# Seven pieces of zeros for an output: three written inside the attention loop, four behind it

## Chip, cores and metric

The kernel runs on one core of a Trainium2 chip. The metric is the device time of one execution in microseconds (us); smaller is better.

## What is computed

Two steps follow each other. The first is a decaying linear attention over 4 batches, 8 heads, 768 positions and head size 64; the second is a mixture of experts, in which each of the 3,072 resulting rows of 512 values goes through its two best of eight experts.

```python
for t in range(S):
    state = gamma * state + einsum('bhd,bhe->bhde', k[:, :, t], v[:, :, t])
    y[:, :, t] = scale * einsum('bhd,bhde->bhe', q[:, :, t], state)
x = y as rows of (batch, position), 512 wide
logits = x @ w_gate + log1p(exp(x @ w_noise)) * noise
top2 = the two largest of 8 logits; top2_w = their softmax
for e in range(8):
    for k in range(2):
        mask = top2[:, k] == e
        h = maximum(x[mask] @ w1[e], 0)
        out[mask] += top2_w[mask, k] * (h @ w2[e])
```

## The kernel before

**The attention loop** (lines 758 to 791) goes over 24 chunks of 128 positions, six per batch. For each chunk TensorE makes the scores, the output and the new state, and transposes the rows; the rows go to a DRAM buffer `xbuf` in half precision (`x_store`, line 424). Into the loop's chunks a table of jobs is woven: `at(j, f, ...)` (line 661) puts a job at the end of chunk j. So the loads and conversions of the first experts' weights and the routing of the first three batches (`route_a` to `route_w`) run beside the attention.

**Zeros.** The results of the experts are added into the output by indirect transfers with an add, so the output has to be zero first. A tile `zero` in SBUF holds zeros, and `zero_out(i)` (line 300) writes one piece of the output from it: pieces 0 to 5 are two transfers of 512 KB each (line 304, one for each half of the output), piece 6 is two of 128 KB (line 308). Lines 739 and 740 put the seven pieces at the ends of chunks 12, 14, 16, 18, 20, 21 and 22.

**Behind the loop** (from line 1017) the routing of the last batch runs, while TensorE already works on expert 0: `early(n)` takes the next n units of a list of its matmuls. Around the change the code stands in this order: the gathers and transposes of the rows that batch 2 gave expert 0 (lines 1049 to 1052), the two loads of expert 1's second weights (lines 1054 and 1055, 1 MiB each), then `route_a` to `route_e` of the last batch. In between, `route_w(b - 1)` (line 1070) writes the gate rows of batch 2 from `gateb` into a DRAM table `gbuf` (line 526), and `gates(0, 3, ...)` (line 1071) gathers gate rows from it.

**Queues.** Nothing reorders instructions: each engine runs its own in the order of the code. SP (SyncE) issues loads, stores, zeros, the writes into `gbuf` and the transposes of gathered rows (`x_t`, line 701). GpSimd (POOL) issues all indirect transfers: the gathers of x rows from `xbuf` (`gather`, line 679), of gate rows from `gbuf` (`gates`, line 689) and the adds into the output (`put`, line 964). SP's transfers signal their landing on eight counters in turn (`DMAHW0_49` to `DMAHW7_49`), GpSimd's on eight others (`DMASW0_49` to `DMASW7_49`). Before SP issues a transfer on a counter, it waits until the transfer that used this counter last has landed, which is the one eight places ahead.

**Expert 1** is the first whose products go by `mm1s` (line 872). Its `out_scale` (line 941, called by `hook` at step 11) multiplies the gathered gate rows of all its seven blocks (line 951, VectorE); it needs the last gate gather of expert 1.

Of the kernel before, what the change touches and what calls it, by code (L numbers as in the profile page):

```python
# [96 lines left out]
def moe_kernel(ctx, tc, qT, kT, kt, vt, noise, wgn, w1, w2, ctab, qtab, xbuf, gbuf, out):  # L97
# [22 lines left out]
    def K(n):  # L120
        return ct[:, _C[n][0]:_C[n][1]]
# [178 lines left out]
    def zero_out(i):  # L300

        if i < 6:
            for o in out:
                nc.sync.dma_start(o[128 + i * 512:128 + (i + 1) * 512, :].rearrange("(p r) d -> p r d", p=128),
                                  zero[:, None, :HD].to_broadcast([128, 4, HD]))
        else:
            for o in out:
                nc.sync.dma_start(o[:128, :], zero[:, :HD])
# [139 lines left out]
    def route_a(b):  # L448
        sl = slice(b * NC, (b + 1) * NC)
        nc.vector.tensor_scalar(invp[b % 2].bitcast(I32), upx[:, sl].bitcast(I32), -1.0, float(254 << 23),  # L450
                                op0=OP.mult, op1=OP.add)
        lg = work.tile([128, NC, 2 * E], F32, name="lg")
        nc.vector.tensor_copy(lg, PL[:, :, 1])
        nc.vector.tensor_tensor(lg, lg, PL[:, :, 0], op=OP.add)
        nc.vector.scalar_tensor_tensor(lg, lg, gx, invp[b % 2][:, :, None].to_broadcast([128, NC, 2 * E]),
                                       op0=OP.mult, op1=OP.mult)
        sp = work.tile([128, NC, E], F32, name="sp")
        nc.scalar.activation(sp, lg[:, :, E:], AF.Exp)
        nc.scalar.activation(small.rearrange("p (c e) -> p c e", c=NC), sp, AF.Ln, bias=1.0)
        R[b] = lg  # L460

    def route_b(b):

        lg, sp = R[b], small.rearrange("p (c e) -> p c e", c=NC)
        o = int(b >= B0)
        ny = work.tile([128, NC, NY], F32, name="ny")
        nc.vector.tensor_tensor(sp, sp, nz[:, b * NC:(b + 1) * NC, :], op=OP.mult)
        nc.vector.memset(ny[:, :, 0:1] if o else ny[:, :, E:NY], -3.0e38)
        nc.vector.tensor_tensor(ny[:, :, o:o + E], sp, lg[:, :, :E], op=OP.add)
        oh = work.tile([128, 2, NC, NL], F32, name="oh", bufs=B)  # L470
        m8 = work.tile([128, NC, 8], F32, name="m8")
        i8 = work.tile([128, NC, 8], U32, name="i8")
        for c in range(NC):
            nc.vector.max(m8[:, c, :], ny[:, c, :])
        for c in range(NC):
            nc.vector.max_index(i8[:, c, :], m8[:, c, :], ny[:, c, :])
        R[b] = (oh, m8, i8)
# [183 lines left out]
    def at(j, f, *a):  # L661
        todo.setdefault(j, []).append((f, a))
# [73 lines left out]
    at(23, w_scaled, nc.scalar, 0, "2", 0)  # L736
    at(22, w_load, 1, "1", 0, 2)
    at(22, w_load, 1, "1", 2, 2)
    for i in range(7):
        at((12, 14, 16, 18, 20, 21, 22)[i], zero_out, i)  # L740
    at(2, nc.vector.tensor_copy, lanes16, K("lanes"))
    at(2, nc.vector.tensor_copy, blks16, K("blks"))
    at(2, nc.vector.tensor_copy, lanes.bitcast(F32), lanes16.bitcast(F32))
# [279 lines left out]
    def early(n):  # L1023
        for _ in range(n):
            if units:
                units.pop(0)()
# [28 lines left out]
    w_load(1, "2", 2, 2)  # L1055
    early(1)
    route_a(b)
    early(1)
    route_b(b)
    early(1)  # L1060
# [275 lines left out]
```

## Time and profile before

| what | value |
|---|---|
| median of 3 runs | 647.22 us (646.4 to 648.09) |
| the profiled execution | 647.68 us, its span 645.9 us |
| TensorE busy | 621.1 us, 96% of the span |
| VectorE, ScalarE, GpSimd busy | 446.4, 391.8, 399.3 us |
| moved by DMA | 112.88 MB, mean 175 GB/s |

The loop ends at about 123 us of the span; the rest is the experts. Busy times count instructions of an engine that overlap nothing else of it. Between brackets behind an instruction of the timeline stands how long its engine was idle before it, and what ended that ("issue": nothing that the profile shows). PEclk is the granted clock of TensorE as a share of 2.4 GHz, its other level being 1.2 GHz.

### The profile page before, as it was taken

What the parts mean: (1) busy time and instruction counts of PE and PEld (TensorE: products, weight loads), DVE (VectorE), ACT (ScalarE), POOL (GpSimd) and SP (SyncE); (2) the same over time, 40 slices, a digit from 0 to 9 for tenths busy, and PEclk for the clock granted to TensorE, in tenths of its full rate; (3) what the DMA queues carried; (4) which work ended last, traced back from release to release, by engine and by line L of the source; (5) the groups of instructions that cost most, each with busy time, mean ns of one, the idle gap of its engine ahead of it and who ended that gap; (6) DMA issues with size and microseconds to landing.
All of it is one profiled execution on the core that took longest, in us unless ns stands there. A gap on an engine that the chain in (4) does not pass through costs nothing.

```text
span 645.9 us, 12856 instructions
## 1 busy us (share of the span) xinstructions
PE 621.1 (96%) x4949; PEld 387.3 (60%) x4949; DVE 446.4 (69%) x947; ACT 391.8 (61%) x655; POOL 399.3 (62%) x279
## 2 busy tenths in 40 slices
PE   7999998899899999999999999999999999999995
PEld 4888887655656544654465446544654465445784
DVE  4568988477767799379827983798369656957730
ACT  4687986763356765576547755765576557656311
POOL 3455998254768756884488468736865774583164
PEclk9999999899999999999999999999999999999999
DMA  9899999953955597459745964695477649732043
GB/s 331 314 390 400 352 379 350 303 185 105 214 73 157 86 209 245 51 121 201 206 54 107 253 167 52 112 251 165 54 156 197 165 51 165 187 44 34 6 53 44
DMA packets 107248, 112.88 MB, mean 175 GB/s; under 512 B 64496, under 2 KB 84080, under 8 KB 103600
## 3 DMA queue, kind: packets, MB, share of 16 engines
q1 hardware_dynamic: 86080, 84.29, 44.4%
q0 software_dynamic: 20528, 26.90, 26.0%
q8 instruction: 40, 0.66, 0.4%
q10 hardware_dynamic: 576, 0.84, 0.3%
q14 instruction: 24, 0.20, 0.1%
HBM read 72.16 MB, written 26.47 MB: 153 GB/s over the span
## 4 chain that ended last, share of the span: by engine, by line
PE 81%; DVE 9%; DMA 3%; ACT 2%; POOL 2%; issue 2%; another core or an unknown queue 1%; SPq 0%; POOLq 0%; ACTq 0%
PE pO L990 11%; PE pO L988 10%; PE pO L989 10%; PE pH L889 9%; PE pH L887 9%; PE pH L888 9%; PE pY L378 3%; PE pA L365 3%; PE pY L384 3%; DVE h L904 2%; PE pX L418 2%; PE pU L394 2%; PE pO L979 1%; PE pO L977 1%; PE pO L978 1%
## 5 line engine op out<-in xcount | busy, mean ns | idle before, releaser
L964 POOL DMA_INDIRECT out<-ot,idx x108 | 197.2, 1826 | 144.9 <-ACT ot L958 59.6
L990 PE MATMUL pO<-w2h,h 128*128 128x512 f16 x336 | 127.4, 379 | 2.5 <-DVE h L904 2.5
L988 PE MATMUL pO<-w2h,h 128*128 128x512 f16 x336 | 127.3, 379 | 0.1
L989 PE MATMUL pO<-w2l,h 128*128 128x512 f16 x336 | 127.3, 379 | 0.0
L911 DVE TENSOR_TENSOR s<-pH,s 128x416 f32<-128x416 f32 (+2 forms) x84 | 47.1, 573 | 49.7 <-PE pH L889 32.2
L689 POOL DMA_INDIRECT gx<-gbuf,idx x54 | 61.7, 1142 | 27.7 <-issue 14.6
L679 POOL DMA_INDIRECT xg<-xbuf,idx x55 | 60.0, 1091 | 22.7 <-issue 14.3
L958 ACT ACTIVATE ot<-pO,gse 128x512 f32<-128x512 f32 (+2 forms) x48 | 32.6, 682 | 58.9 <-PE pO L990 54.5
L191 ACT ACTIVATE junk<-wst 128x1024 bf16<-128x1024 f32 x64 | 67.8, 1059 | 0.0
L903 ACT ACTIVATE h<-s 128x832 f16<-128x832 f32 (+2 forms) x42 | 36.3, 872 | 39.9 <-DVE s L911 32.5
L907 ACT ACTIVATE s<-pH 128x416 f32<-128x416 f32 (+2 forms) x84 | 40.3, 508 | 32.6 <-PE pH L889 29.8
L990 PEld LDWEIGHTS <-h 128*128 128x128 f16 x336 | 32.8, 98 | 44.0 <-DVE h L904 5.0
L988 PEld LDWEIGHTS <-h 128*128 128x128 f16 x336 | 32.9, 98 | 38.7 <-ACT h L903 0.6
L887 PE MATMUL pH<-xt,wsh 128*128 128x416 f16 (+2 forms) x168 | 56.0, 333 | 0.2 <-DVE h L904 0.2
L989 PEld LDWEIGHTS <-h 128*128 128x128 f16 x336 | 32.9, 98 | 38.8
L889 PE MATMUL pH<-xt,wsl 128*128 128x416 f16 (+2 forms) x168 | 56.0, 333 | 0.0
L888 PE MATMUL pH<-xt,wsh 128*128 128x416 f16 (+2 forms) x168 | 56.0, 333 | 0.0
L220 DVE SCALAR_TENSOR_TENSOR w2l<-wst,wsc,w2h 128x1024 f16<-128x1024 f32 x28 | 35.8, 1279 | 14.1 <-ACT w2h L215 10.0
L338 POOL TENSOR_TENSOR vp<-in_v,ct 128x512 f32<-128x512 f32 x24 | 25.0, 1043 | 31.0 <-issue 16.8
L904 DVE SCALAR_TENSOR_TENSOR h<-s,h 128x832 f16<-128x832 f32 (+2 forms) x42 | 41.5, 990 | 2.3 <-ACT h L903 2.3
L845 ACT ACTIVATE xt<-s 128x832 f16<-128x832 f32 (+2 forms) x28 | 24.5, 874 | 28.6 <-DVE s L844 28.3
L372 DVE TENSOR_TENSOR am<-pA,ct 128x512 f32<-128x512 f32 x48 | 30.9, 684 | 14.6 <-PE pA L365 12.1
(216 smaller groups left out, 1489.8 us busy)
## 6 DMA issues: line engine op xcount, KB each, us to landing
wst<-w SPq DMA_DIRECT2D x28, 1024.0 KB
in_q<-qT SPq DMA_DIRECT2D x24, 256.0 KB
in_k<-kT SPq DMA_DIRECT2D x24, 256.0 KB
in_v<-vt SPq DMA_DIRECT2D x24, 256.0 KB
xbuf<-xr SPq DMA_DIRECT2D x24, 256.0 KB
out<-zero SPq DMA_DIRECT2D x12, 512.0 KB
in_kt<-kt SPq DMA_DIRECT2D x20, 256.0 KB
wst<-w SPq DMA_DIRECT2D x8, 512.0 KB
```

The lines of the kernel that those rows point to most:

```text
L191: nc.scalar.activation(junk, st[:, i * 1024:(i + 1) * 1024], AF.Square, accum_out=ss[:, i:i + 1])
L679: nc.gpsimd.indirect_dma_start(out=x[:p1], out_offset=None, in_=xbuf[:128 + rows], in_offset=bass.IndirectOffsetOnAxis(ap=idx[:p1, i:i + 1 ...
L689: nc.gpsimd.indirect_dma_start(out=GX[e][:, t, :], out_offset=None, in_=gbuf[:128 + rows], in_offset=bass.IndirectOffsetOnAxis(ap=idx[:, i ...
L887: nc.tensor.matmul(p, wh, bh[:, k, :], start=start and k == 0, stop=False, skip_group_check=True)
L888: nc.tensor.matmul(p, wh, bl[:, k, :], start=False, stop=False, skip_group_check=True)
L889: nc.tensor.matmul(p, wl, bh[:, k, :], start=False, stop=(k == 1), skip_group_check=True)
L904: wait.append(lambda: nc.vector.scalar_tensor_tensor(lo, src, 0.0, hi, op0=OP.max, op1=OP.subtract))
L911: nc.vector.tensor_tensor(s[:, u], p, s[:, u], op=OP.add)
L964: nc.gpsimd.indirect_dma_start(out=out[s], out_offset=bass.IndirectOffsetOnAxis(ap=idx[:n, i:i + 1], axis=0), in_=ot[:n, s * HD:(s + 1) * ...
L988: nc.tensor.matmul(p, a, WT["2h"][:, f, :], start=(f == 0), stop=False)
L989: nc.tensor.matmul(p, a, WT["2l"][:, f, :], start=False, stop=False)
L990: nc.tensor.matmul(p, c, WT["2h"][:, f, :], start=False, stop=(f == FT - 1))
```

## The change

Three pieces of zeros stay in the loop, now at the ends of chunks 12, 15 and 18. The other four (three pairs of 512 KB and the pair of 128 KB) are issued behind the loop, after `route_a` of the last batch.

```diff
@@ -736,8 +736,8 @@
     at(23, w_scaled, nc.scalar, 0, "2", 0)
     at(22, w_load, 1, "1", 0, 2)
     at(22, w_load, 1, "1", 2, 2)
-    for i in range(7):
-        at((12, 14, 16, 18, 20, 21, 22)[i], zero_out, i)
+    for i in range(3):
+        at((12, 15, 18)[i], zero_out, i)
     at(2, nc.vector.tensor_copy, lanes16, K("lanes"))
@@ -1055,6 +1055,8 @@
     w_load(1, "2", 2, 2)
     early(1)
     route_a(b)
+    for i in range(3, 7):
+        zero_out(i)
     early(1)
     route_b(b)
```

The order of SP at the loop's end, before: `x_store` (L424), the transposes of expert 0's first rows (L701), zeros (L304, L308) and the loads of expert 1's first weights (L187).

```order
L304 DMA out<-zero 512x1x256 [waits DMAHW6_49]
L304 DMA out<-zero 512x1x256 [waits DMAHW7_49]
L424 DMA xbuf<-xr 128x1024 [waits DMAHW0_49,Activation_49]
L701 DMA_TRANSPOSE xe<-xg 128x8x128 [waits DMAHW1_49,DMASW0_49]
L701 DMA_TRANSPOSE xe<-xg 128x8x128 [waits DMAHW2_49,DMASW1_49]
L701 DMA_TRANSPOSE xe<-xg 128x8x128 [waits DMAHW3_49,DMASW2_49]
L304 DMA out<-zero 512x1x256 [waits DMAHW4_49]
L304 DMA out<-zero 512x1x256 [waits DMAHW5_49]
L424 DMA xbuf<-xr 128x1024 [waits DMAHW6_49,Activation_49]
L187 DMA wst_2217<-w 128x2048 [waits DMAHW7_49,Pool_49]
L187 DMA wst_2217<-w 128x2048 [waits DMAHW0_49]
L308 DMA out<-zero 128x256 [waits DMAHW1_49]
```

The same place of SP now:

```order
L424 DMA xbuf<-xr 128x1024 [waits DMAHW3_49,Activation_49]
L424 DMA xbuf<-xr 128x1024 [waits DMAHW4_49,Activation_49]
L701 DMA_TRANSPOSE xe<-xg 128x8x128 [waits DMAHW5_49,DMASW0_49]
L701 DMA_TRANSPOSE xe<-xg 128x8x128 [waits DMAHW6_49,DMASW1_49]
L701 DMA_TRANSPOSE xe<-xg 128x8x128 [waits DMAHW7_49,DMASW2_49]
L424 DMA xbuf<-xr 128x1024 [waits DMAHW0_49,Activation_49]
L187 DMA wst_2211<-w 128x2048 [waits DMAHW1_49,Pool_49]
L187 DMA wst_2211<-w 128x2048 [waits DMAHW2_49]
```

The zeros around the transposes and behind the weight loads are gone from here; the rest keeps its order.

The order of SP behind the loop, before: the transposes of expert 0's next rows, the loads of expert 1's second weights, the write of the gate table (L526), the next transposes.

```order
L701 DMA_TRANSPOSE xe<-xg 128x8x128 [waits DMAHW7_49,DMASW6_49]
L701 DMA_TRANSPOSE xe<-xg 128x8x64 [waits DMAHW0_49,DMASW7_49]
L187 DMA wst_2419<-w 128x2048 [waits DMAHW1_49,Pool_49]
L187 DMA wst_2419<-w 128x2048 [waits DMAHW2_49]
L526 DMA gbuf<-gateb 128x6x10 [waits DMAHW3_49,DVE_49]
L701 DMA_TRANSPOSE xe<-xg 128x8x64 [waits DMAHW4_49,DMASW1_49]
```

The same place of SP now:

```order
L187 DMA wst_2411<-w 128x2048 [waits DMAHW1_49,Pool_49]
L187 DMA wst_2411<-w 128x2048 [waits DMAHW2_49]
L304 DMA out<-zero 512x1x256 [waits DMAHW3_49]
L304 DMA out<-zero 512x1x256 [waits DMAHW4_49]
L304 DMA out<-zero 512x1x256 [waits DMAHW5_49]
L304 DMA out<-zero 512x1x256 [waits DMAHW6_49]
L304 DMA out<-zero 512x1x256 [waits DMAHW7_49]
L304 DMA out<-zero 512x1x256 [waits DMAHW0_49]
L308 DMA out<-zero 128x256 [waits DMAHW1_49]
L308 DMA out<-zero 128x256 [waits DMAHW2_49]
L526 DMA gbuf<-gateb 128x6x10 [waits DMAHW3_49,DVE_49]
L701 DMA_TRANSPOSE xe<-xg 128x8x64 [waits DMAHW4_49,DMASW1_49]
```

Eight zeros now stand between the weight loads and the write of the gate table. That write waits on the same counter as before, which the first of these zeros now holds. The order of every other engine is unchanged.

## Rows read from the trace of the kernel before

**Rows 1.** The page, busy us of each engine (share of the span, instructions).

```profile
PE 621.1 (96%) x4949; PEld 387.3 (60%) x4949; DVE 446.4 (69%) x947; ACT 391.8 (61%) x655; POOL 399.3 (62%) x279
```

**Rows 2.** Stretches: us, busy us of each engine, PEclk, DMA share, GB/s.

```profile
90.00:100.00 10.00, 10.00 (x179) 9.05 (x179) 9.69 (x35) 7.59 (x17) 10.00 (x7) 1.00 1.05 383
...
105.00:110.00 5.00, 3.64 (x54) 2.90 (x51) 2.44 (x10) 1.69 (x3) 4.33 (x5) 1.00 1.12 264
110.00:115.00 5.00, 2.75 (x46) 2.30 (x44) 2.98 (x11) 4.03 (x8) 3.78 (x4) 1.00 1.08 302
115.00:120.00 5.00, 4.00 (x53) 3.73 (x54) 3.11 (x15) 2.90 (x6) 0.00 (x0) 0.75 1.07 290
120.00:125.00 5.00, 5.00 (x57) 4.02 (x54) 2.90 (x10) 4.61 (x7) 0.00 (x0) 0.91 1.05 348
...
140.00:145.00 5.00, 5.00 (x33) 2.57 (x29) 3.26 (x16) 4.97 (x11) 0.00 (x0) 1.00 0.84 280
145.00:150.00 5.00, 5.00 (x26) 2.42 (x25) 4.79 (x21) 0.79 (x3) 0.00 (x0) 1.00 0.50 175
...
180.00:185.00 5.00, 3.71 (x34) 3.03 (x32) 1.93 (x4) 2.31 (x7) 3.70 (x3) 1.00 0.49 56
```

**Rows 3.** Timeline of TensorE: start, us, instruction, [idle before <-what ended it].

```profile
116.00 0.19 PE L499 MATMUL pL<-mb,trib 128*128 128x60 bf16 x1 [2.92 <-DVE p2m L167]
...
182.41 0.27 PE L811 MATMUL pH<-xe,w1h 128*128 128x256 f16 x1 [1.20 <-DVE h L815]
...
219.30 0.34 PE L887 MATMUL pH<-xt,wsh 128*128 128x416 f16 x1 [0.17 <-DVE h L904]
```

**Rows 4.** Timeline of GpSimd from 150 to 215 us.

```profile
150.20 0.97 POOL L689 DMA_INDIRECT gx<-gbuf,idx  x1 [11.74 <-DMA gbuf<-gateb]
154.16 1.74 POOL L679 DMA_INDIRECT xg<-xbuf,idx  x1 [2.99 <-DVE idx L594]
156.21 0.94 POOL L679 DMA_INDIRECT xg<-xbuf,idx  x1 [0.30 <-issue]
...
158.68 1.97 POOL L679 DMA_INDIRECT xg<-xbuf,idx  x1 [0.30 <-issue]
...
170.00 1.23 POOL L679 DMA_INDIRECT xg<-xbuf,idx  x1 [2.08 <-DMA gbuf<-gateb]
171.53 1.64 POOL L964 DMA_INDIRECT out<-ot,idx  x1 [0.30 <-issue]
...
213.60 0.98 POOL L689 DMA_INDIRECT gx<-gbuf,idx  x1 [0.30 <-issue]
```

**Rows 5.** Timeline of VectorE at expert 1's out_scale.

```profile
215.99 0.17 DVE L951 TENSOR_TENSOR gm<-gx,onef 128x7 f32<-128x7 f32 x1 [0.83 <-DMA gx<-gbuf,idx]
```

**Rows 6.** Timeline of SP's issues: start, us, line, transfer, how many.

```profile
103.21 1.85 SPq L304 DMA_DIRECT2D out<-zero  x2
...
116.06 1.27 SPq L304 DMA_DIRECT2D out<-zero  x2
...
140.05 1.00 SPq L187 DMA_DIRECT2D wst<-w  x2
146.12 0.38 SPq L526 DMA_DIRECT2D gbuf<-gateb  x1
```

**Rows 7.** Transfers: packets and rate from 60 to 100 us, then sizes by issue.

```profile
DMA packets 10078, 14.91 MB, mean 373 GB/s; under 512 B 1559, under 2 KB 4684, under 8 KB 10069
...
out<-zero SPq DMA_DIRECT2D x12, 512.0 KB
...
out<-zero SPq DMA_DIRECT2D x2, 128.0 KB
```

**Rows 8.** Waits of GpSimd from 130 to 220 us: total, times, longest.

```profile
POOL out L964 <- DMA out<-ot,idx: 2.4, 2, 1.6
```

## The prediction

> **What bounds the kernel now.** I read the shares of the engines first: TensorE is busy for 621.1 of 645.9 us [rows 1], so only what makes it idle, or what lowers its clock, can move the time by much. Then I read the table by stretches [rows 2], to see where it idles near the two places that the change touches. Inside the loop it does not: from 90 to 100 us TensorE is busy 10.00 of 10 us, while the DMA engines are full (share 1.05, 383 GB/s). At the loop's end it does: from 105 to 120 us it is busy 3.64, 2.75 and 4.00 of 5 us each, so 1.36 + 2.25 + 1.00 = 4.61 us are idle, the longest piece 2.92 us before 116.00 [rows 3]. Behind that pause the granted clock is 0.75 and 0.91 of 2.4 GHz in two stretches of 5 us [rows 2]; the part spent at the lower level of 1.2 GHz costs 5 x 0.25 + 5 x 0.09 = 1.7 us. So 6.3 us are lost there.
>
> Behind the loop the chain that matters is GpSimd's. Its queue runs in order: a gather of gate rows at 150.20 that waited for the write of the gate table into `gbuf`, then from 154.16 on gathers of x rows, adds into the output and gate gathers almost without a pause, up to the last gate gather at 213.60 [rows 4]. On that one VectorE waits 0.83 us at 215.99 [rows 5], and TensorE waits 0.17 us for VectorE at 219.30 [rows 3]. There is no slack at the end of this chain: what makes GpSimd late there makes TensorE late by as much.
>
> **The change part by part.** It adds no work and removes none: 14 transfers of zeros before, 14 after.
>
> *Three pieces stay in the loop, at chunks 12, 15 and 18.* I cost this at nothing: TensorE covers it, busy 10.00 of 10 us with full DMA engines [rows 2]. If that cover were gone, each pair of issues would hold SP for 1.27 us [rows 6].
>
> *The pieces at the loop's end go.* 1 MiB issued at 103.21, 1 MiB at 116.06 and the small pair behind it [rows 6] no longer stand in the queue while TensorE idles. The gain lies between 0 and the 6.3 us. For a gain: the DMA share is 1.12, 1.08 and 1.07 in just these stretches [rows 2]. Against: it is 1.05 at 90 to 100 us without any pause, and at 180 to 185 us TensorE is idle for 1.29 us at a share of 0.49 [rows 2], 1.20 of it in a wait on VectorE [rows 3]. The trace names no transfer as what ended the idle time at the loop's end. I take a third, 2.1 us, since the nearest rows (90 to 100 us) speak against the DMA engines as the cause.
>
> *Eight transfers now stand on SP behind the two weight loads of 140.05.* By the issue times of 1.27 us for two, they take 5.1 us, from 141.05 to 146.1. SP was idle then, waiting for the gate table until 146.12 [rows 6], so the issuing itself is hidden. What is not hidden is the eight landing counters that SP's transfers share in turn: the seventh zero now waits for the first weight load to land, the eighth for the second, and the write into `gbuf`, next in the queue, for the first zero.
>
> *The bytes.* Six transfers of 512 KB and two of 128 KB [rows 7] are 3.41 MB. At the 373 GB/s that a stretch with many zeros moved [rows 7] they take 9.1 us. The two weight loads keep the DMA engines busy until about 147.5: from 145 to 150 us the share is 0.50 [rows 2]. The zeros then fill them until 156.6.
>
> *The write into `gbuf`.* Before, it was issued at 146.12 [rows 6] and released GpSimd at 149.90 (the gather began at 150.20 after its usual 0.30 us [rows 4]), 3.8 us after its issue and 2.4 us after the weights were through. Now it is issued at about 150.4 (147.5, one zero of 1.4 us, some 1.5 us to land). If it overtakes the zeros it lands 3.8 us later, at 154.2; if it comes behind them, at 156.6 + 2.4 = 159.0. I take 159.0, since before, too, it landed only once the transfers issued ahead of it were through. The Trainium skill ("DMA: Bandwidth & Descriptors", section "Queues, rings and completion order") says that a DMA engine consumes the descriptors of one queue in ring order and takes turns between queues; no run here shows it for this write, and by it the sum is the one with 159.0, without it the one with 154.2.
>
> *GpSimd's chain.* Behind 159.0 stand 0.30 us, the gate gather of 0.97 us and 0.30 us, so the first gather of x rows starts at 160.6 where it started at 154.16 [rows 4]: 6.4 us late. Some of it comes back: the gathers at 154.16 and 158.68 took 1.74 and 1.97 us where the one at 156.21 took 0.94 [rows 4], beside VectorE's large operations of that time; I take off 1.2 us, between 0 (slow again) and 1.8 (both at 0.94). The pauses later in the chain do not take up the rest: the 2.08 us before 170.00 [rows 4] are, by the counters that the program waits on there, a wait for a gather buffer that the transposes of GpSimd's own earlier gather must free (the row names another transfer that landed last), and the 2.4 us before adds [rows 8] are waits for its own earlier adds. They move along. So 5.2 us of delay reach the last gate gather, VectorE's wait and TensorE's: +5.2 us.
>
> *The clock behind the new pause.* After 2.92 us of idle time the clock fell at a cost of 1.7 us [rows 2, 3]; a pause of 5.2 us should do the same: +1.7 us, at least 0.
>
> *What is hidden.* The adds into the output may start only when all zeros have landed; the first one is at 171.53 [rows 4], 12 us behind my 159.0. The weights that the zeros follow are ahead of them in the queue.
>
> **The sum.** The profiled execution took 647.68 us, 0.46 above the median of 647.22. 647.68 - 2.1 + 5.2 + 1.7 = 652.5, against the median 652.0 us. What one measurement can tell from no change is about 0.3%, 1.9 us.
>
> **The rivals.**
> 1. *The write into `gbuf` overtakes the zeros, and the loop's end is what pays* (faster). The full queue made the pauses of 105 to 120 us, so up to 6.3 us come back, while the write at 154.2 starts the gathers at 155.8, 1.6 us late and 0.4 after the part that comes back: 647.2 - 6.3 + 0.4 = 641.3, or 645.3 where only 2.3 us come back. It decides as soon as the relief exceeds the delay by 1.9 us. For it: the DMA shares above 1 in those stretches. Against: no row names a transfer there. Chance 0.15.
> 2. *Both are large* (the same). The loop's end gives all 6.3 us, the chain takes 5.2 and perhaps the clock's 1.7: 646.1 to 647.8. Together with the case that neither is felt (no relief and 0.4 late, 647.6) I give it 0.19.
> 3. *Nothing comes back at all* (slower still). No relief at the loop's end, GpSimd 6.4 late, the clock down: 647.2 + 6.4 + 1.7 = 655.3. For it: 1.20 us of idle time at 182.41 with half-empty DMA engines. Chance 0.12.
> 4. *The change doesn't do what it says*: the rows of SP show the eight zeros where the diff puts them, so I give this none.
>
> **How the numbers follow.** My forecast, 652.0 with 649.5 to 654.1 around it, has 0.54. Slower is the forecast and rival 3: 0.66. The same is 0.19, faster 0.15. The range of 645.0 to 655.5 takes in rivals 2 and 3 and the upper edge of rival 1; it leaves out most of rival 1 and a tail above, under 0.2 together.
>
> **What the changed profile would show.** Right: GpSimd's gate gather at about 159 instead of 150.20, waiting for the `gbuf` write; the first gather of x rows near 160; VectorE's wait on the gate rows grown from 0.83 to some 6 us; a TensorE pause near 219 with a lower granted clock behind it; 105 to 120 us with a little less idle time. Wrong: a gate gather before 155, or a chain that has caught up by the last gate gather, or TensorE busy through 105 to 120 us at full clock.

## The result, and the profile after

In the first set of runs the change makes the kernel slower: 654.53 us against 648.53 us before (medians of 20 runs each on one chip), a ratio of 1.0088 [1.0062, 1.0114]. The forecast was 652.0 us, slower, with a range of 645.0 to 655.5. The profiled execution took 654.32 us, its span 652.5 us.

That ratio is not the same in every set of runs. Each set was made on one chip, with the kernel before beside it; again, again2 and again3 were made on three different chips, and the chip of the first result is not on record. A fifth set, on a further chip, is used further down and has no run of the unaltered change. The ratios are of fast runs alone (within 1.5% of the kernel's fastest) and are not the quotients of the medians, which here are 1.0093, 0.9999, 0.9999 and 1.0130.

| set | before, median us | change, median us | ratio |
|---|---|---|---|
| first result | 648.53 | 654.53 | 1.0088 [1.0062, 1.0114] |
| again | 642.76 | 642.69 | 1.0011 [0.9981, 1.0042] |
| again2 | 642.24 | 642.15 | 1.0022 [0.9999, 1.0046] |
| again3 | 645.45 | 653.86 | 1.0132 [1.0114, 1.015] |

The stretches after, answering to [rows 2] (us, busy us of PE, PEld, DVE, ACT, POOL, PEclk, DMA share, GB/s):

```profile
100.00:105.00 5.00, 4.38 (x73) 3.80 (x72) 3.35 (x30) 4.26 (x10) 3.14 (x4) 1.00 0.89 236
105.00:110.00 5.00, 4.03 (x66) 3.50 (x66) 4.12 (x15) 2.58 (x6) 4.51 (x6) 1.00 0.98 228
110.00:115.00 5.00, 3.61 (x64) 3.11 (x62) 2.69 (x12) 3.92 (x9) 1.77 (x2) 1.00 0.94 223
115.00:120.00 5.00, 5.00 (x70) 4.04 (x66) 3.76 (x15) 5.00 (x8) 0.17 (x1) 1.00 0.99 388
165.00:170.00 5.00, 3.79 (x16) 1.32 (x15) 3.32 (x16) 1.24 (x3) 0.95 (x2) 1.00 1.11 162
170.00:175.00 5.00, 3.67 (x23) 2.82 (x24) 2.12 (x10) 1.42 (x3) 2.46 (x3) 0.76 1.18 243
```

TensorE's timeline, answering to [rows 3]:

```profile
134.40 0.19 PE L499 MATMUL pL<-mb,trib 128*128 128x60 bf16 x1 [0.54 <-DVE mb L486]
...
171.33 0.27 PE L811 MATMUL pH<-xe,w1h 128*128 128x256 f16 x1 [2.18 <-DMA xe<-xg]
...
220.23 0.34 PE L887 MATMUL pH<-xt,wsh 128*128 128x416 f16 x1
...
286.32 0.34 PE L887 MATMUL pH<-xt,wsh 128*128 128x416 f16 x1 [1.88 <-DVE h L904]
```

GpSimd's timeline and VectorE's wait, answering to [rows 4] and [rows 5]:

```profile
154.72 0.97 POOL L689 DMA_INDIRECT gx<-gbuf,idx  x1 [21.63 <-DMA gbuf<-gateb]
155.99 0.95 POOL L679 DMA_INDIRECT xg<-xbuf,idx  x1 [0.30 <-issue]
...
214.65 0.98 POOL L689 DMA_INDIRECT gx<-gbuf,idx  x1 [0.30 <-issue]
```

```profile
216.92 0.17 DVE L951 TENSOR_TENSOR gm<-gx,onef 128x7 f32<-128x7 f32 x1 [0.72 <-DMA gx<-gbuf,idx]
```

SP's issues, answering to [rows 6]:

```profile
134.67 1.00 SPq L187 DMA_DIRECT2D wst<-w  x2
135.72 10.50 SPq L304 DMA_DIRECT2D out<-zero  x6
146.27 2.37 SPq L308 DMA_DIRECT2D out<-zero  x2
148.74 0.83 SPq L526 DMA_DIRECT2D gbuf<-gateb  x1
```

The routing of each batch has the same first matmul on TensorE (L499). For the first and the last batch it stands before at

```profile
57.56 0.19 PE L499 MATMUL pL<-mb,trib 128*128 128x60 bf16 x1 [0.25 <-DVE p2m L167]
...
139.79 0.19 PE L499 MATMUL pL<-mb,trib 128*128 128x60 bf16 x1 [0.54 <-DVE mb L486]
```

and after, for the first batch, at

```profile
55.25 0.19 PE L499 MATMUL pL<-mb,trib 128*128 128x60 bf16 x1 [0.25 <-DVE p2m L167]
```

Up to there the two kernels issue the same, so the profiled execution before was 2.3 us late already when the change began to act. At the last batch the distance is 5.4 us (139.79 against 134.40). The relief of this pair is the difference, 3.1 us.

Three more things are to be seen. The loop's end lost 4.61 us of idle time from 105 to 120 us and 1.7 us by the clock before; now 0.62 + 0.97 + 1.39 us are idle from 100 to 115 and the clock stays at 1.00. The eight zeros hold SP from 135.72 to 148.64, so the write into `gbuf` goes out at 148.74, 2.6 us later than before, although the weight loads ahead of it go out 5.4 us earlier (2.3 of them by the late start of the profile before); GpSimd waits 21.63 us for it instead of 11.74. And the place where the delay reaches TensorE is not 219 us: from 165 to 175 it is idle for 1.21 + 1.33 us, 2.18 us of it on transposed rows, with the clock at 0.76 behind that.

VectorE's operation on the gate rows stands at 216.92 instead of 215.99 [rows 5], and TensorE's matmul of 219.30 before [rows 3] at 220.23. So TensorE goes from 5.4 us ahead to 0.9 us behind: the delay costs 6.3 us up to here, and 5.7 of the 6.6 us between the spans arise behind it. In sum, 6.6 = -2.3 (late start before) - 3.1 (relief) + 6.3 (delay) + 5.7 (later experts). In the later experts TensorE has seven pauses of over 0.7 us: 1.88 us before 286.32, and 0.73, 1.11, 1.06, 1.07, 0.84 and 1.17 us at 362, 364, 428, 429, 486 and 550 us. Before has two, of 0.80 and 0.89 us.

### The profile page after: what moved, and what is told of

Its sections match the earlier page's. It is cut to its first block, busy times and chain, and to the rows that moved or that the text cites. A ratio compares the mean times of both kernels' runs of the same rounds, so it can differ in the third digit from the quotient of the medians.

```text
span 652.5 us, 12856 instructions
## 1 busy us (share of the span) xinstructions
PE 621.4 (95%) x4949; PEld 385.1 (59%) x4949; DVE 445.2 (68%) x947; ACT 391.8 (60%) x655; POOL 398.4 (61%) x279
## 4 chain that ended last, share of the span: by engine, by line
PE 75%; DVE 9%; DMA 5%; ACT 4%; SPq 3%; issue 2%; POOL 1%; another core or an unknown queue 1%; POOLq 0%; DVEq 0%; ACTq 0%
PE pO L990 10%; PE pO L988 9%; PE pO L989 9%; PE pH L887 9%; PE pH L889 9%; PE pH L888 9%; PE pY L378 2%; PE pA L365 2%; PE pY L384 2%; DVE h L904 2%; SPq L304 2%; DVE am L372 2%; PE pO L979 1%; PE pO L977 1%; PE pO L978 1%
## 5 line engine op out<-in xcount | busy, mean ns | idle before, releaser
L964 POOL DMA_INDIRECT out<-ot,idx x108 | 201.1, 1862 | 147.0 <-ACT ot L958 68.3
L689 POOL DMA_INDIRECT gx<-gbuf,idx x54 | 59.8, 1108 | 37.6 <-DMA gbuf<-gateb 21.6
L679 POOL DMA_INDIRECT xg<-xbuf,idx x55 | 57.1, 1039 | 23.5 <-issue 14.6
```

Of the source, the lines that this page charges most:

```text
L679: nc.gpsimd.indirect_dma_start(out=x[:p1], out_offset=None, in_=xbuf[:128 + rows], in_offset=bass.IndirectOffsetOnAxis(ap=idx[:p1, i:i + 1 ...
L689: nc.gpsimd.indirect_dma_start(out=GX[e][:, t, :], out_offset=None, in_=gbuf[:128 + rows], in_offset=bass.IndirectOffsetOnAxis(ap=idx[:, i ...
L964: nc.gpsimd.indirect_dma_start(out=out[s], out_offset=bass.IndirectOffsetOnAxis(ap=idx[:n, i:i + 1], axis=0), in_=ot[:n, s * HD:(s + 1) * ...
```

## Experiments

### The unaltered change on other chips: again, again2, again3

> The changed kernel once more, unaltered. Theory A (the four pieces hold up the write into gbuf behind the loop, and GpSimd's chain makes TensorE late): the time is 0.6 to 1.2% above before; the gate gather starts at 153 to 160 us of the span, and TensorE idles again between 160 and 176 us. If the pauses of TensorE at 286, 361 and 428 us of the first profile are due to the change, they stand there again (1.0 to 1.9 us each); if they are chance, they are gone or stand elsewhere. Rival B (the loss is made of these later pauses): TensorE is level with before at 220 us and loses 4 us or more behind it.

> The changed kernel once more, to see which of its two results holds: 1.0088 of before at first, 1.0011 in the repeated run. If the difference lay in pauses of TensorE behind 280 us, which the first profile shows (7.9 us in seven pauses of over 0.7 us) and the second doesn't, this run shows again one or the other, with 1.006 to 1.011 where they are there and 0.998 to 1.004 where not. The pause of 4 to 5 us between 160 and 190 us and the gate gather at 152 to 155 are expected in both.

> The changed kernel a fourth time. So far it stood at 1.0088 of before where before itself took 648.5 us and GpSimd's adds (L964, 235 to 600 us) 1.90 us each, and at 1.0011 and 1.0022 where before took 642.8 and 642.2 us and the adds 1.78 and 1.81 us. If the delay costs more where GpSimd's adds are slower, as there GpSimd has less room to catch up in the experts: with before above 647 us and adds above 1.85 us the ratio is 1.005 to 1.011 and TensorE pauses again behind 280 us; with before near 642 us and adds near 1.8 us it is 0.999 to 1.004. If the first result was chance, the ratio is 1.000 to 1.003 whatever before takes.

The ratios are in the table above. SP's issues and GpSimd's gate gather in again:

```profile
134.18 10.34 SPq L304 DMA_DIRECT2D out<-zero  x6
144.57 2.50 SPq L308 DMA_DIRECT2D out<-zero  x2
147.16 0.89 SPq L526 DMA_DIRECT2D gbuf<-gateb  x1
```

```profile
153.01 0.97 POOL L689 DMA_INDIRECT gx<-gbuf,idx  x1 [21.46 <-DMA gbuf<-gateb]
```

VectorE's and TensorE's timelines and the stretches of again:

```profile
182.04 1.03 DVE L837 TENSOR_TENSOR s<-xe 128x832 f32<-128x832 f16 x1 [7.41 <-DMA xe<-xg]
182.98 0.42 DVE L815 SCALAR_TENSOR_TENSOR h<-pH,h 128x256 f16<-128x256 f32 x1
```

```profile
167.04 0.27 PE L811 MATMUL pH<-xe,w1h 128*128 128x256 f16 x1 [1.45 <-DMA xe<-xg]
...
183.46 0.39 PE L990 MATMUL pO<-w2h,h 128*128 128x512 f16 x1 [2.11 <-DVE i L944]
...
219.21 0.34 PE L887 MATMUL pH<-xt,wsh 128*128 128x416 f16 x1
```

```profile
180.00:185.00 5.00, 2.17 (x10) 0.60 (x7) 2.89 (x8) 0.00 (x0) 3.43 (x3) 1.00 0.93 152
185.00:190.00 5.00, 2.85 (x7) 0.93 (x8) 3.77 (x7) 3.68 (x5) 4.08 (x3) 0.58 0.46 52
190.00:200.00 10.00, 10.00 (x95) 5.88 (x93) 8.53 (x10) 3.81 (x6) 8.47 (x6) 0.87 0.82 243
```

This is the route by which a late GpSimd reaches TensorE in these two runs. The late gathers make the transposes of expert 1's rows late. VectorE's first sum over these rows (L837) waits 7.41 us for them at the head of its queue, and the operations that finish expert 0's results (L815, L944) stand behind it. TensorE's second products of expert 0 wait for them, and then for ScalarE's L814 (2.11, 1.13 and 1.74 us): from 180 to 190 us it is busy 2.17 + 2.85 of 10 us, and the clock is 0.58 in the second half and 0.87 in the 10 us behind. In again2 the same operation waits 6.46 us. In the first profile it waits 1.55 us and in again3 not at all, so there the lost time takes other ways, among them the direct wait for transposed rows. The gate gather (153.01 and 153.05) came where the two runs expected it. The time of again, expected 0.6 to 1.2% above before, did not, and of its pause only 1.45 us stand between 160 and 176 us; again2, which expected it between 160 and 190, had both right.

Neither of these two has a pause of 0.7 us behind 280 us. Again3 has five there (1.26, 1.10, 0.82, 1.11 and 1.05 us) and the ratio 1.0132, above what was expected of it, with a before of 645.45 where over 647 was expected. GpSimd's adds from 235 to 600 us took 1,875 ns there, 1,900 in the first profile, 1,780 and 1,805 in again and again2. So the large ratios go with pauses in the later experts. These pauses are not the change's alone: on the two chips of again and again2 TensorE is idle for 0.1 us behind 225 us in every profile, whatever the kernel, and in the profiles of the other sets it is idle in every kernel, for 3.6 us in the kernel before and 9.1 with the change in the first pair, and on the chip of before_again for 4.7 us in the kernel before, 5.5 in e7_gates_ahead, which has no late write, and 5.6 in e8_sums_later, which has one. What makes them, and whether the change adds to them, is open. That slower adds are their cause is not shown: the next kernel, on the chip of again, has 1,844 ns and no such pause.

### The zeros behind the write: e1_after_write

```diff
     route_a(b)
-    for i in range(3, 7):
-        zero_out(i)
...
     route_w(b - 1)
+    for i in range(3, 7):
+        zero_out(i)
     gates(0, 3, (B - 1) * S)
```

> The four pieces are issued behind the write into gbuf instead of ahead of it. Theory A: the gate gather starts near 146 us instead of 154.7, the first gather of x rows near 149, TensorE does not idle between 163 and 176 us, the relief at the loop's end stays; 0.3 to 0.8% below before. Rival B (the full DMA engines between 137 and 153 us do it, whatever stands in the queue): as slow as the changed kernel, 0.5% or more above before. Rival C (the transposes of expert 0's last rows, now the ones behind the zeros, are held up as the write was): TensorE idles before 175 us as in the changed kernel, within 0.4% of before.

638.61 us beside 642.76 before: 0.9913 [0.9884, 0.9942]. GpSimd's gate gather, VectorE's wait and TensorE's pause in this kernel:

```profile
144.52 0.97 POOL L689 DMA_INDIRECT gx<-gbuf,idx  x1 [12.22 <-DMA out<-zero]
```

```profile
210.60 0.17 DVE L951 TENSOR_TENSOR gm<-gx,onef 128x7 f32<-128x7 f32 x1 [4.05 <-DMA gx<-gbuf,idx]
```

```profile
213.92 0.51 PE L887 MATMUL pH<-xt,wsh 128*128 128x416 f16 x1 [3.37 <-DVE h L904]
```

By the ratio the gain, 0.87%, is above the expected 0.3 to 0.8%, by the medians, 0.65%, within it. The gate gather starts 8.5 us earlier than in again, on the same chip, with the same bytes moved a few lines later. From 160 to 190 us TensorE has no pause left. What appears instead is a pause at 213.92, behind VectorE's wait for the last gate gather: the chain that the prediction priced ends exactly there, once nothing stops TensorE earlier. This pause takes back part of what the earlier write saves. The same matmul stands at 219.21 in again, without a wait; the one ahead of it at 210.21 here and at 219.03 in again, 8.8 us apart, while the spans, 637.0 and 640.8 us, are 3.8 us apart. The other 5.0 us go with the pause and with the granted clock behind it, 0.88 and 0.78 in the two stretches of 5 us from 210 us.

### The zeros left out: e2_left_out

```diff
-    for i in range(3, 7):
-        zero_out(i)
```

Pieces 3 to 6, 3.25 MiB of the output, are not zeroed in this kernel.

> The four pieces are left out: 3.25 MiB of the output are not zeroed. This measures the relief at the loop's end alone. Theory A: TensorE gains about 3 to 5 us by 125 us and keeps them; 0.4 to 0.9% below before. Rival B (the loop's end gains nothing that lasts): within 0.3% of before.

638.92 us, 0.9913 [0.9881, 0.9946]; the gate gather:

```profile
143.12 0.97 POOL L689 DMA_INDIRECT gx<-gbuf,idx  x1 [11.40 <-DMA gbuf<-gateb]
```

Leaving the zeros out is worth no more than putting them behind the write, as far as these runs can tell (0.3%). Behind the write their bytes cost nothing that shows; ahead of it they do.

### The zeros inside the loop's last stores: e3_at_once

```diff
     lctx.close()
+    for i in range(3, 7):
+        zero_out(i)
...
     route_a(b)
-    for i in range(3, 7):
-        zero_out(i)
```

> The four pieces are issued right behind the loop, at about 115 us, ahead of the weights' second loads; they should be through before 132 us, in a stretch where the DMA engines of the changed kernel are a third busy or less. Theory A: as with the pieces left out, 0.4 to 0.9% below before. Rival D (the stores of the last x rows and the transposes behind them are held up): a TensorE pause between 125 and 150 us, within 0.3% of before or above.

638.17 us, 0.9899 [0.9865, 0.9932]; the gate gather at 145.39. All three kernels without the zeros ahead of the write lie within 0.8 us. Against before they gain 0.87 to 1.01% by the ratios, 5.6 to 6.5 us, and 3.8 to 4.6 us by the medians: that is what the relief at the loop's end is worth when it isn't given back. Against again on this chip the write held behind the zeros costs 1.0011 - 0.9913, 0.98% or 6.3 us, by the ratios, each of which is uncertain by 0.3%; by the medians, 642.69 against 638.61, it costs 4.1 us, and by the spans of the two profiles 3.8.

### The write by another queue: e4_write_by_act

```diff
-        nc.sync.dma_start(gbuf[128 + b * S:128 + (b + 1) * S, :]...
+        (nc.scalar if b == B - 2 else nc.sync).dma_start(gbuf[128 + b * S:128 + (b + 1) * S, :]...
```

> As the changed kernel, but the one write into gbuf that stands behind the eight zeros is issued by ScalarE instead of SP. Theory A (SP's own queue holds it: in the repeated run of the change SP was busy issuing the eight zeros from 134.2 to 147.1 us, so the write could be issued only then): the write goes out when VectorE has the rows, near 139.5, and the gate gather starts near 143 to 146 instead of 153; TensorE loses no 5 us between 160 and 190, and the time is that of the kernel with the zeros behind the write, about 0.991 of before. Theory B (the DMA engines are full, whichever queue issues): the gate gather stays at 151 to 154 and the time at 1.000 to 1.009 of before.

641.35 us beside 642.24 before, 0.9988 [0.9965, 1.0012]. Issue by ScalarE, the gate gather, and the transfers of 128 to 160 us (KB each, us to landing):

```profile
139.25 0.39 ACTq L526 DMA_DIRECT2D gbuf<-gateb  x1
```

```profile
148.40 0.98 POOL L689 DMA_INDIRECT gx<-gbuf,idx  x1 [16.83 <-DMA out<-zero]
```

```profile
gbuf<-gateb ACTq DMA_DIRECT2D x1, 30.0 KB, 8.4
```

Both theories miss. The write is free of SP's queue and goes out at 139.25, but lands only 8.4 us later; the gather starts at 148.40, between the 143.12 without zeros (e2_left_out, on another chip) and the 153.05 of again2 on the same chip. So half of the delay is SP's, and half is the way through DMA engines that are full of zeros. The Trainium skill ("DMA: Bandwidth & Descriptors", section "Queues, rings and completion order") says that the write which reports a transfer's end lands only after every earlier write of the same DMA engine, across its queues. These 8.4 us agree with it in size: the write landed at 147.65, beside the third zero (issued at 135.82, 12.0 us to landing), the last one whose issue had ended when the write went out. ScalarE paid too: it waited for the rows to write, and TensorE paused 1.74 us at 142.12 behind it.

### Half of the zeros ahead: e5_half

```diff
-    for i in range(3, 7):
+    for i in range(3, 5):
         zero_out(i)
...
     route_w(b - 1)
+    for i in range(5, 7):
+        zero_out(i)
```

> As the changed kernel, but only pieces 3 and 4 (four zeros of 512 KB) stand ahead of the write into gbuf; pieces 5 and 6 come right behind it. Theory A (SP is held for as long as the bytes ahead take): 2 MiB of weights and 2 MiB of zeros from 133.1 us at 373 GB/s are through at 144.3, so the write goes out at 142 to 144 and the gate gather starts at 146 to 148; the time lies between 0.991 and 1.001 of before. Theory C (the eight shared counters alone hold it, as the prediction had it: the seventh and eighth zero wait for the weights, the write for the first zero): with four zeros the write's counter is free, it goes out at 139.5 and the gate gather starts at 143 to 145; the time is 0.991 of before.

641.86 us, 0.9978 [0.9953, 1.0002]. SP's issue of the write, its landing (KB each, us to landing), and the gate gather:

```profile
139.89 2.34 SPq L526 DMA_DIRECT2D gbuf<-gateb  x1
```

```profile
gbuf<-gateb SPq DMA_DIRECT2D x1, 30.0 KB, 10.1
```

```profile
150.70 0.97 POOL L689 DMA_INDIRECT gx<-gbuf,idx  x1 [18.83 <-DMA out<-zero]
```

Both miss the gather again (the time lies in theory A's wide range), and theory C falls: with four zeros the write goes out at 139.89, as C has it, and still the gather starts at 150.70. It is not the issue that is late here but the landing, 10.1 us behind it. What fits is a write that lands last in its queue, whenever it was issued. The weights and four zeros, 4.19 MB from 133.6 us at the 342 GB/s of these stretches, are through at about 145.9; with no zeros ahead the write took 3.5 us from issue to release (e2_left_out, 139.37 to 142.82), which gives an estimate of 149.4, and the gather 0.30 later at 149.7. The same estimate for again, 5.51 MB from 133.1 us at 357 GB/s (338, 363 and 370 in the stretches of 5 us from 135 us on), gives 152.3, where the gather started at 153.01. The gather stands at 143.1, 150.7 and 153.0 us with none, four and eight zeros ahead.

### Only the spacing: e6_spacing

```diff
-        at((12, 14, 16, 18, 20, 21, 22)[i], zero_out, i)
+        at((12, 15, 18, 18, 20, 21, 22)[i], zero_out, i)
```

> The kernel before, with only the second and third piece moved, from chunks 14 and 16 to 15 and 18; the other four stay at 18, 20, 21 and 22, none is behind the loop. If the relief at the loop's end comes from the zeros that left it: the time is that of before (0.998 to 1.002) and TensorE idles 4 to 5 us between 105 and 120 us as before. If it came from the spacing, or if the pauses of the profiled execution before were chance: about 2 us of idle time there, and a time of 0.993 to 0.996 of before.

644.2 us beside 642.24, 0.9984 [0.995, 1.0019]. The time is that of before within 0.5%, so the spacing of the pieces that stay is worth nothing that shows, and the relief comes from those that leave.

### The kernel before once more: before_again

> The kernel before, unaltered, for a second profile of it. Time: 0.997 to 1.003 of before. If its lost time at the loop's end is a property of the kernel, TensorE loses 4 to 5 us between 105 and 140 us more than the kernels without zeros there, either as in the first profile (2.92 us before the routing's matmul at 116 and a lower clock) or as in the run with only the spacing changed (0.97 us for transposed rows and 2.14 us before the routing's matmul at 137); the loads of expert 1's first weights go out near 118 instead of 110.5, and the gate gather starts at 147 to 150 instead of 143 to 145.

646.94 us beside 650.65, 0.997 [0.9925, 1.0016]. The gate gather starts at 146.90. SP, TensorE at the last batch's routing, and the stretches there:

```profile
108.96 4.07 SPq L701 DMA_TRANSPOSE xe<-xg  x3
116.45 2.00 SPq L187 DMA_DIRECT2D wst<-w  x2
```

```profile
135.99 0.19 PE L499 MATMUL pL<-mb,trib 128*128 128x60 bf16 x1 [2.14 <-DVE mb L486]
```

```profile
130.00:135.00 5.00, 3.86 (x24) 2.21 (x23) 3.77 (x28) 1.37 (x5) 2.96 (x2) 1.00 0.70 184
135.00:140.00 5.00, 4.01 (x21) 2.08 (x21) 3.33 (x19) 2.99 (x7) 0.00 (x0) 0.68 0.77 247
```

The same rows on the same chip in the next kernel, which has the zeros where the change puts them:

```profile
106.62 4.17 SPq L701 DMA_TRANSPOSE xe<-xg  x3
111.66 0.73 SPq L187 DMA_DIRECT2D wst<-w  x2
```

```profile
134.55 0.19 PE L499 MATMUL pL<-mb,trib 128*128 128x60 bf16 x1 [0.55 <-DVE mb L486]
```

```profile
130.00:135.00 5.00, 4.45 (x34) 2.67 (x33) 3.77 (x32) 1.75 (x6) 3.06 (x2) 1.00 0.53 138
135.00:140.00 5.00, 5.00 (x28) 2.53 (x26) 3.42 (x16) 4.84 (x10) 0.00 (x0) 1.00 0.86 269
```

With zeros at the loop's end the transposes go out 2.3 us later and expert 1's weight loads 4.8 us later; TensorE waits 2.14 us instead of 0.55 before the last batch's routing, and from 130 to 140 us it loses 1.14 + 0.99 us and 1.6 us by the clock, against 0.55 us. So in this pair, 3.2 us in all, the relief stands behind SP's queue, in the routing at 135 us. In the first pair it does not: there the same matmul waits 0.54 us in both kernels, and the 3.1 us arise between 100 and 120 us; the pause before the routing's matmul of batch 2 differs most (2.92 us before 116.00 [rows 3], 1.13 us after). That pause need not be the zeros': in before_again only 1.02 us stand there, and in e7_gates_ahead, which has no zeros ahead of that point but the three of the loop, 2.70 us do:

```profile
113.26 0.19 PE L499 MATMUL pL<-mb,trib 128*128 128x60 bf16 x1 [2.70 <-DVE p2m L167]
```

### VectorE's sums moved: e8_sums_later

```diff
     for n in range(FT):
         mm1(0, SECOND, CAPS[0], n)
...
-        if n > 3:
-            xs1(1)
...
-            xs1(4)
+            xs1(8)
```

> The changed kernel with VectorE's first four sums of expert 1's rows (L837, which wait for the transposes) taken out of expert 0's last matmul groups and put behind them. Theory A (GpSimd's delay reaches TensorE because these sums stand in VectorE's queue ahead of expert 0's own results: waits of 6 to 7 us on L837 in both repeated runs of the change): the 5 us that TensorE loses between 180 and 190 us go; the 1.5 to 2.7 us near 167, a direct wait for transposed rows, stay; GpSimd's last gate gather then makes TensorE wait near 215 to 219 as the prediction had it, 3 to 5 us. The time is 0.994 to 1.002 of before. Rival (the pause comes from ScalarE or from the gate rows of expert 0 instead): TensorE still loses 4 to 5 us between 178 and 190 and the time is 1.000 to 1.004.

656.77 us beside 650.65, 1.011 [1.0043, 1.0177], slower than the 0.994 to 1.002 expected. VectorE's operation on the gate rows, TensorE behind it, and the stretches:

```profile
218.91 0.17 DVE L951 TENSOR_TENSOR gm<-gx,onef 128x7 f32<-128x7 f32 x1 [7.28 <-DMA gx<-gbuf,idx]
```

```profile
222.22 0.51 PE L887 MATMUL pH<-xt,wsh 128*128 128x416 f16 x1 [6.61 <-DVE h L904]
```

```profile
180.00:190.00 10.00, 10.00 (x49) 4.57 (x48) 7.24 (x11) 4.92 (x7) 7.65 (x4) 1.00 0.65 105
```

The mechanism is as expected: from 180 to 190 us TensorE is busy all the time, and the lost time moves to 222 us, 6.61 us behind a wait of VectorE of 7.28 us for the gate rows. That is the picture that the prediction drew for 219 us, with more lost than the 3 to 5 us expected here. Not all of that is the late write: in this profile GpSimd also waits 4.21 us for an earlier add of its own before 197.17, and its last gate gather starts at 216.58, where again has 210.20. The unaltered change was not measured on this chip. With L837 in its usual place, TensorE pays earlier.

### Gate gathers ahead: e7_gates_ahead

The zeros stand where e3_at_once has them, and in addition:

```diff
-        for i in ((0, 1), (2, 3, 4), (5, 6))[n]:
+        for i in ((0, 1, 2, 3), (4, 5, 6), ())[n]:
             gates(1, i)
```

> As the kernel with the four pieces right behind the third last store of the loop (0.990 of before), and expert 1's seven gate gathers each one block earlier in GpSimd's order (four at the first block, three at the second), so that the last stands ahead of the adds of the second block. That kernel's only pause of over 0.8 us behind the loop is 2.70 us before 212.8, behind VectorE's wait of 3.37 us for the last gate gather, with the granted clock at 0.92 to 0.95 behind it. Theory A (GpSimd's order is the bound there): the last gate gather starts near 202 instead of 207, the pause and the lower clock go, and the time falls by 3 to 4 us, to 0.984 to 0.987 of before. Rival: the adds behind the gathers hold output buffers longer and TensorE pauses as long elsewhere: 0.988 to 0.992.

645.05 us beside 650.65, 0.9935 [0.9895, 0.9975], where 0.984 to 0.987 was expected. TensorE is busy 15.00 of 15 us from 200 to 215 and has no pause at 213 any more, but the last gate gather starts only at 207.25, and other pauses stand at 113 us (above) and behind 410 us. Against e3_at_once, measured on another chip, the intervals overlap, so no further gain is shown. Both beat the kernel before.

## Why the prediction was right, and where not

**The forecast held, partly by other terms.** Slower, and 652.0 us against 654.53; the sum had -2.1 + 5.2 + 1.7. The first pair of profiles had -3.1 and +6.3 for these terms, and two more that no term names: -2.3 from a late start of the execution before, +5.7 from the later experts.

**Three pieces in the loop cost nothing**: right (e6_spacing, 0.9984 with 1 in its interval; the first pair keeps its distance of 2.3 us up to 100 us).

**The relief of 2.1 us: mis-sized, too small.** The failing step is "the nearest rows speak against the DMA engines as the cause", from which a third of the gain was taken. The two pairs of profiles give 3.1 and 3.2 us, the three kernels without the delay 3.8 to 4.6 us by their medians and 5.6 to 6.5 by their ratios. The sum priced idle time of TensorE at 105 to 120 us. What both pairs share is that the transposes and the weight loads behind the zeros in SP's queue go out earlier; where TensorE gains from it differs (100 to 120 us in the first pair, 130 to 140 in before_again against e8_sums_later). That the queue's order is the cause is argued from this and not shown by an edit of that order alone.

**SP's issuing hidden, 5.1 us: wrong.** Eight zeros took SP 12.9 us in again (134.18 to 147.07). The duration of 1.27 us for two came from a place where SP had no 2 MiB of loads just ahead [rows 6].

**The eight counters**: not what decides. In e5_half the write's counter was free and the gather still late.

**The bytes and the write behind them: right in size.** The prediction had the gate gather 9.1 us late (159.3 against 150.20); again against e2_left_out has 9.9 us (153.01 against 143.12), and on the chip of before_again it is 8.1 us (154.97 in e8_sums_later against 146.90 before). The first gather of x rows was to be 6.4 us late and is 154.29 against 148.00 in e1_after_write, 6.3 us. The rival in which the write overtakes the zeros fails with this.

**The delay and its clock, 5.2 + 1.7 = 6.9 us: near in the first pair (6.3), too large as a net cost on the chip of again (4.1 by the medians, 6.3 by the ratios), and wrong in place.** "There is no slack at the end of this chain" holds for the kernel without the delay too: there, with the relief, TensorE waits 3.37 us for the last gate gather (e1_after_write), and a delay that TensorE pays earlier takes this wait away. And "reach the last gate gather, VectorE's wait and TensorE's" overlooked earlier readers of the late rows: the sums of L837 in VectorE's queue, and the matmuls of expert 0 on transposed rows (1.45 us at 167.04 in again, 2.18 at 171.33 in the first profile). TensorE paid there, and by 216 us GpSimd had caught up with it. Two of the signs that the prediction named against itself came true, "a chain that has caught up by the last gate gather" and, by 0.3 us, "a gate gather before 155" (154.72). The pause that it expected appeared in the changed kernel only once the sums were moved (e8_sums_later).

**The first add hidden**: right, it starts at 174.43, 20 us behind the release of the gate gather by the write that followed the zeros, after 0.30 us of idle time that no transfer ended.

**What the sum lacked.** On the chip of again the two terms nearly cancel (-4.1 and +4.1 us by the medians, -5.6 and +6.3 by the ratios), and there rival 2, both large and the same time, is what happened. In the first result 5.7 us came behind 216 us, in the later experts, and stood in no term of the sum or of a rival; why they differ from set to set is open. That the forecast fits the first result is to that extent luck.

## What to carry to other kernels

A transfer on a queue costs what stands behind it in the queue: large stores that nobody waits for belong behind the small write that everybody waits for, and here their bytes then cost nothing that shows (0.9913 against 1.0011 of before for moving four calls by a few lines). When a chain is made late, look for the first reader of its data on every in-order engine, not for the place where it is tight today; and ask what the kernel without the delay would wait for next, since the net cost is smaller by that. And where a whole-kernel time differs by 1% from chip to chip, size the terms within one set of runs.

## What was not expected of the hardware

SP was held while it issued zeros behind 2 MiB of loads. The first zero of again took 0.59 us to issue; all six took 10.34 us, so the other five took 1.95 us each on average, and the fourth alone 2.93. In e1_after_write, with only the small write between loads issued 6 us before and the zeros, all six took 7.11 us.

In one profile results are picked up late. In again3 ScalarE's evacuations of expert 0's first products (L814) follow each other by 3.0 to 3.6 us, each behind a wait for TensorE, while TensorE's last matmul before the first of these gaps had started at 178.20 and lasted 0.27; in again2 the same operations follow each other by 1.3 us (172.66, 173.98, 175.28). Again3:

```profile
179.30 0.38 ACT L814 ACTIVATE h<-pH 128x256 f16<-128x256 f32 x1 [2.81 <-PE pH L813]
182.91 0.38 ACT L814 ACTIVATE h<-pH 128x256 f16<-128x256 f32 x1 [2.19 <-PE pH L813]
```

TensorE lost 1.72, 2.14 and 1.34 us in these gaps, and the trace names nothing that ended the first two. Its cause stays open, and so does why the kernel before takes from 642.2 to 650.7 us in the five sets of runs.
